# Messages, stores and sums of an attention stage sent in another order

## The chip, the cores and the metric

The kernel runs on one core of a Trainium2 chip. The metric is the device time of one execution in microseconds (us). The core's engines work side by side, each through its own list of instructions in order: PE (matrix products, with PEld for its weight loads), DVE, ACT and POOL (elementwise work) and SP, which here only issues DMAs and passes messages.

## The reference

```python
# attention, for each of 4 x 8 heads: 1152 keys, 64 wide
q_pool = q.reshape(B, H, S // 2, 2, D).mean(axis=3)          # 576 queries
scores = scale * np.matmul(q_pool, k.transpose(0, 1, 3, 2))  # 576 x 1152
attn = np.exp(scores - np.max(scores, axis=-1, keepdims=True))
attn = attn / (np.sum(attn, axis=-1, keepdims=True) + 1e-09)
x = np.matmul(attn, v)      # then the heads side by side: 2304 rows of 512
# first MoE block (dense): h = x @ w_in, g of h by pieces, x = g @ w_out (512 -> 2048 -> 512)
# second MoE block: each row to its best expert of 8, out = gate * (relu(x @ w1) @ w2)
```

## The kernel before

Attention takes the first 447 us of 1120; the two MoE blocks follow and are the same in both kernels. Its 32 heads go in 16 pairs, and a pair in nine steps of 128 queries; `s` counts all 144 steps, `t = s % 9` the steps of a pair, and step `t = 4` holds queries of both heads and has 18 score matmuls instead of 9. In a step PE makes the scores of 128 queries against 1152 keys into a PSUM tile `sc`, of which there is one (L238). DVE scales them into `e` and takes the peak of each row in the same instruction (L265). ACT takes the exponentials and their sums (L272). Two steps later PE transposes `e` in 64-wide pieces into `pa` and `pb` (L289); ACT and DVE split these into a high and a low part, `pth` and `ptl` (L307, L309), since every product is made of a few such parts. PE then multiplies them with `v` (L322, in four groups of 288 queries for a pair, of 36 half-row matmuls each), beside the scores of later steps. POOL splits q, k and v of the next pair (L180 to L214) and issues the loads of k.

All these matmuls use half the rows of the PE array (`UP` and `LO`), so that two run beside each other. Where both halves add into one PSUM bank, the second half's last part must come after the first half's end. `relay` (L254) sees to it with a nop on SP: the nop waits for the first half's last matmul, and the other half's matmul waits for the nop. This text calls it a message. Each step has one for the scores and one for the transposes; each group of L322 has one more.

SP takes its list in order, and the DMAs that it issues stand in the same list: loads of q (L153) and v (L165), stores of the products (`av_b` and `av_t`, L364), of the reciprocals of the sums (`rs_b`, L354) and loads of weights for the MoE block (L512, L517). `later` puts a DMA on a list with the step from which it may go, and at the end of each step `send` issues two of those that are due, or three at `t = 3` and in the last pair. `sums` (L344 to L354) makes the reciprocals of one pair's sums, transposes them on DVE and queues four small stores.

In the first three steps `warm` (L220) adds transposes whose result nobody reads: 22, 12 and 10 (`WARM`, L52). `load_first` (L132) loads q and k of the first two heads.

Near attention's end the MoE block's input `x` is read back from the stores. `tail` queues these loads: `xth` and `rows` with the upper and lower half of the products, `xtl` with the reciprocals, in two halves of 2 x 128 rows of the input, and a fifth part, `row`. POOL adds and multiplies them (L657, L658, L662), then issues the weights' third block (`raw`, L512). `h` of the MoE block (L692) follows on PE.

## Time and profile before

| | |
|---|---|
| three runs | 1118.53, 1121.33, 1123.40 us; median 1121.33 |
| profiled execution | 1121.47 us; span 1119.8 us |
| busy share of the span | PE 97%, PEld 89%, DVE 76%, ACT 67%, POOL 39% |
| DMA | 132.01 MB, mean 118 GB/s |
| granted TensorE clock | 0.993 of full speed, mean of the span |

The profile is of one execution, and its times are counted from the start of its span. A wait is idle time of an engine; behind the arrow stands what ended it, and `SPq L254` there is a message. The chain of waits goes back from the last instruction to whatever released each one. A row that begins with a number is an instruction or several of one kind in sequence, with the start and the duration.

### The profile page before, as it was taken

Reading aid. Unit: us, or ns where it says so; the run is one execution under the profiler, and the core shown is the slowest. Engines: PE = TensorE matmul, PEld = TensorE weight load, DVE = VectorE, ACT = ScalarE, POOL = GpSimd, SP = SyncE. Lnnn points to the kernel's source line nnn. Section 1 sums busy time; section 2 is a strip of 40 time slices with the busy share of each in tenths; the row PEclk is TensorE's granted clock in tenths of the full one; section 3 lists DMA queues with packets and bytes.
Section 4 is the critical chain, followed back from the end, with each engine's and each line's share of the span. In section 5 each row is a group of like instructions: output and inputs, shape, how many; then the busy total and the mean of one; then the engine's idle time right before and its main releaser. Section 6 shows DMA issues by size and latency. Waiting matters only on the chain.

```text
span 1119.8 us, 27167 instructions
## 1 busy us (share of the span) xinstructions
PE 1088.0 (97%) x10276; PEld 998.8 (89%) x10276; DVE 852.2 (76%) x1620; ACT 754.9 (67%) x1432; POOL 441.6 (39%) x473
## 2 busy tenths in 40 slices
PE   8999999999999998999999999999999999999997
PEld 7999989999889998999999989998889889988887
DVE  5999999999999995798757745663545866677775
ACT  4999989998898986555554445444446456577664
POOL 5988778778778848000021121101020231122211
PEclk8999999999999999999999999999999999999999
DMA  6445545446545435665132213210341121286544
GB/s 162 119 126 135 154 121 138 130 121 161 140 121 135 115 118 129 204 196 172 55 113 59 65 29 99 59 32 21 104 145 54 30 86 40 88 280 218 168 147 126
DMA packets 76854, 132.01 MB, mean 118 GB/s; under 512 B 21031, under 2 KB 39079, under 8 KB 76704
## 3 DMA queue, kind: packets, MB, share of 16 engines
q1 hardware_dynamic: 67856, 103.48, 31.9%
q0 software_dynamic: 8544, 26.31, 8.0%
q8 instruction: 88, 1.44, 0.6%
q14 instruction: 62, 0.51, 0.2%
q10 hardware_dynamic: 304, 0.26, 0.1%
HBM read 140.08 MB, written 20.08 MB: 143 GB/s over the span
## 4 chain that ended last, share of the span: by engine, by line
PE 73%; DVE 14%; issue 5%; POOL 2%; SPq 2%; DMA 2%; ACT 2%; POOLq 0%; DVEq 0%; ACTq 0%
PE h L692 18%; PE y L724 18%; PE sc L238 9%; DVE e L265 9%; PE d_po L1401 8%; PE d_ph L1367 7%; PE av L322 6%; DVE ptl L309 3%; PE pa L289 2%; PE d_ph L1381 1%; SPq L364 1%; DMA out<-d_ob,d_rec 1%; PE pb L289 1%; PE d_pt L1346 1%; POOL kT L193 1%
## 5 line engine op out<-in xcount | busy, mean ns | idle before, releaser
L265 DVE TENSOR_SCALAR_CACHE_REDUCE e<-sc 128x1152 f32<-128x1152 f32 x144 | 194.6, 1352 | 26.2 <-PE sc L238 23.1
L238 PE MATMUL sc<-kT,qt 64*128 64x384 f32 x1440 | 191.6, 350 | 18.5 <-DVE e L265 14.1
L272 ACT ACTIVATE e<-e,nm 128x1152 f32<-128x1152 f32 x144 | 182.2, 1265 | 8.6 <-DVE e L265 8.1
L238 PEld LDWEIGHTS sc<-kT,qt 64*128 64x128 f32 x1440 | 148.3, 187 | 35.9 <-DVE e L265 26.0
L1307 DVE TENSOR_TENSOR e<-e,e 128x512 fp32r<-128x512 f32 x200 | 129.9, 688 | 27.0 <-ACT e L1306 11.4
L322 PE MATMUL av<-pth,vh 64*128 64x288 f32 x1152 | 145.2, 311 | 2.3 <-SPq L254 2.2
L322 PE MATMUL av<-ptl,vh 64*128 64x288 f32 x1152 | 143.2, 311 | 0.0
L711 DVE SCALAR_TENSOR_TENSOR u<-h,u 128x320 f32<-128x320 f32 (+1 forms) x112 | 55.8, 498 | 113.3 <-ACT u L710 113.3
L309 DVE TENSOR_TENSOR ptl<-pa,pth 128x768 fp32r<-128x768 f32 x144 | 137.3, 953 | 4.3 <-ACT pth L307 3.4
L707 ACT ACTIVATE u<-h,half 128x320 f32<-128x320 f32 (+1 forms) x112 | 59.7, 533 | 118.5 <-PE h L692 116.9
L307 ACT CAST pth<-pa 128x768 fp32r<-128x768 f32 x144 | 114.9, 798 | 34.7 <-PE pa L289 32.3
L322 PEld LDWEIGHTS av<-pth,vh 64*128 64x128 f32 x1152 | 119.3, 186 | 4.3 <-SPq L254 4.3
L1401 PE MATMUL d_po<-e,e 128*128 128x512 f32 x504 | 120.6, 392 | 0.0
L322 PEld LDWEIGHTS av<-ptl,vh 64*128 64x128 f32 x1152 | 117.6, 186 | 0.0
L1306 ACT CAST e<-e 128x512 fp32r<-128x512 f32 x200 | 113.8, 620 | 0.3 <-issue 0.3
L724 PE MATMUL y<-wh,gh 128*128 128x512 f32 x288 | 113.9, 395 | 0.0
L724 PE MATMUL y<-wh,gl 128*128 128x512 f32 x288 | 113.7, 395 | 0.0
L724 PE MATMUL y<-wl,gh 128*128 128x512 f32 x288 | 113.6, 394 | 0.0
L1401 PEld LDWEIGHTS d_po<-e,e 128*128 128x128 f32 x504 | 92.8, 188 | 18.0
L289 PE MATMUL pb<-idf,e 64*128 64x64 f32 x864 | 100.6, 223 | 0.3
L657 POOL TENSOR_TENSOR xl<-xth,xl 128x512 f32<-128x512 f32 (+1 forms) x9 | 11.8, 1315 | 224.4 <-DMA xl<-av_b 127.2
L713 ACT CAST gh<-u 128x320 fp32r<-128x320 f32 (+1 forms) x112 | 52.4, 468 | 66.2 <-DVE u L711 66.1
(253 smaller groups left out, 2386.8 us busy)
## 6 DMA issues: line engine op xcount, KB each, us to landing
e<-moe_w SPq DMA_DIRECT2D x104, 512.0 KB
qr<-q SPq DMA_DIRECT2D x62, 288.0 KB
kr<-k POOLq DMA_DIRECT2D x60, 192.0 KB, 3.4
vr<-v SPq DMA_DIRECT2D x16, 576.0 KB
av_b<-avs SPq DMA_DIRECT2D x64, 128.0 KB
raw<-moe_w_in SPq DMA_DIRECT2D x14, 512.0 KB
raw<-moe_w_out SPq DMA_DIRECT2D x14, 512.0 KB
yt<-emb_rows SPq DMA_DIRECT2D x24, 256.0 KB
```

The source lines that it names most:

```text
L238: i = nc.tensor.matmul(s[:, j, 0:384], lhsT=qt[p, w, c:c + 128], rhs=d["kT", h][p, r], start=start, stop=stop)
L265: self.nc.vector.tensor_scalar(out=e.rearrange("p (a b) -> p a b", a=3), in0=d["sc"][:, :, 0:384], scalar1=-0.5 / D ** 0.5, scalar2=None, ...
L272: self.nc.scalar.activation(e, e, AF.Exp, bias=d["nm"][:, t:t + 1], scale=-1.0, accum_out=d["sum"][:, t:t + 1])
L289: x = nc.tensor.transpose(o, e[p, i * 128:(i + 1) * 128], idf[p, p])
L307: nc.scalar.copy(hi, p)
L309: nc.vector.tensor_sub(out=lo, in0=p, in1=hi.bitcast(F32))
L322: m = nc.tensor.matmul(box["t"][:, 0:GQ], lhsT=self.vh[p, h * 9 + i % 9], rhs=r[p, i % 9, c0:c0 + GQ], start=half == i == 0, stop=half == ...
L692: nc.tensor.matmul(ps[:, :n], lhsT=a[:, k], rhs=b[:, k, h0:h0 + n], start=i == 0, stop=i == 11)
L724: self.nc.tensor.matmul(y, lhsT=a, rhs=b, start=j == 0 and q == 0, stop=j == NF - 1 and q == 2)
L1306: self.nc.scalar.copy(hi, r)
L1307: self.nc.vector.tensor_sub(out=lo, in0=r, in1=hi.bitcast(F32))
L1401: self.nc.tensor.matmul(self.o, lhsT=(self.hh, self.hl)[a][f // 4][:, f % 4, s], rhs=self.w[b, f // 2][:, f % 2], start=f == 0 and q == 0, ...
```

## The change

The DMAs of attention go on two lists, stores first. One DMA is sent behind the scores' message, in the middle of the step, and one behind the transposes' message (two at `t = 3`, and at `t = 1` to `4` of the last pair). The reciprocals of two pairs are made together, behind the odd pair. At the start q of the second head and v of the first pair are loaded behind the first scores, k of the second head goes first, POOL's splits of the second head's q come a step later, and `WARM` has five portions. At attention's end the last transposes go into `sc`, and the last two groups of L322 become matmuls of whole rows, behind everything else (`av_all`). `tail` is called before the second `send` of its step, and the upper half of x is loaded in one piece of 512 x 512, with its reciprocals, ahead of both pieces of the lower half. ACT's and POOL's operations at the end follow in another order.

```diff
-WARM = 22, 12, 10
+WARM = 22, 12, 12, 8, 8
...
-    def later(self, step, f):
-        self.queue.append((step, f))
+    def later(self, step, f, queue=None):
+        (self.queue if queue is None else queue).append((step, f))
 
     def send(self, n):
-        out = [x for x in self.queue if x[0] <= self.step][:n]
-        for x in out:
-            self.queue.remove(x)
-            x[1]()
+        for q in (self.stores, self.queue):
+            out = [x for x in q if x[0] <= self.step][:n]
+            n -= len(out)
+            for x in out:
+                q.remove(x)
+                x[1]()
...
         if h:
-            parts = [(kr, ks), (qr, (q, q))]
+            parts = [(kr, ks)] if which == "k" else [(d["qr", h], (q, q))]
...
-    def turn(self, n, t):
+    def turn(self, n, t, late=False):
...
+        if late:
+            sc = self.ps_s.tile([128, 3, 512], F32, name="sc")
+            pa, pb = sc[:, 0:2], sc[:, 2:3]
...
+    def av_all(self, n, g):
+        h, c = g // 2, slice(g * GQ, g * GQ + GQ)
+        t = self.ps_v.tile([128, 512], F32, name="av", tag="av")
+        for i in range(18):
+            self.nc.tensor.matmul(t[:, 0:GQ], lhsT=self.vh[:, h * 9 + i % 9],
+                                  rhs=(self.pth if i < 9 else self.ptl)[:, i % 9, c], start=i == 0, stop=i == 17)
+        self.nc.scalar.copy(self.avs[:, c], t[:, 0:GQ])
+        if g % 2:
+            self.store(n, h)
...
     def sums(self, n):
 
         nc = self.nc
         del self.st[n]
+        if n % 2 == 0:
+            return
         b, hp = divmod(n, 4)
         rt = self.sm.tile([128, 32], F32, name="rt")
-        nc.vector.reciprocal(self.r[:, 0:9], self.r[:, 0:9])
+        nc.vector.reciprocal(self.r[:, 0:18], self.r[:, 0:18])
         nc.vector.transpose(rt, self.r)
...
         for c in range(4):
-            self.later(self.step + 1, lambda c=c: nc.sync.dma_start(out=out[c], in_=rt[32 * c:32 * c + 9]))
+            self.later(self.step + 1, lambda c=c: nc.sync.dma_start(out=out[c], in_=rt[32 * c:32 * c + 18]))
...
-                            self.later(s + (m > 1 and n == 0) * 4, lambda a=(m, h, p): self.load_q(*a))
-                if s < 3:
+                            self.later(s + (m > 1 and n == 0) * 3, lambda a=(m, h, p): self.load_q(*a))
+                if s < len(WARM):
                     self.warm(WARM[s])
                 up, lo = self.scores(n, t)
             for a in ready.get(s, []):
-                self.av_group(*a)
-            count = 18 if s > nt + 1 else 6 if t in (2, 3, 4) else 9
+                if a < (np_ - 1, 2):
+                    self.av_group(*a)
+            count = 18 if s >= nt else 6 if t in (2, 3, 4) else 9
...
             if s < nt:
                 self.peak(n, t)
+            if s == 0:
+                self.load_first(1, "q")
+                self.load_v(0)
+            self.send(1)
             if 2 <= s < nt + 2:
-                (a, b), ps = self.turn(*divmod(s - 2, 9))
-                if s >= nt:
-                    av(1, 4)
+                (a, b), ps = self.turn(*divmod(s - 2, 9), s > nt)
+                if s == nt:
+                    av(1, 7)
...
             go = s >= nt - 7 and len(g) > 0 and g[0][0]()
-            self.send(3 if t == 3 or n + 1 >= np_ else 2)
-            while any(min(left[half], len(self.avq[half])) for half in range(2)):
+            if s == nt - 9:
+                self.prep.release()
+                g.extend(tail())
+            self.send(2 if t == 3 or not more and 0 < t < 5 else 1)
+            while s != nt and any(min(left[half], len(self.avq[half])) for half in range(2)):
...
-            if s == nt - 1:
+            if s == nt + 1:
                 self.ps_s.release()
                 early()
-            if s == nt - 9:
-                self.prep.release()
-                g.extend(tail())
+                for a in range(2, 4):
+                    self.av_all(np_ - 1, a)
...
+                m1.x_raw(0, (slice(0, 4), 0, 512), lambda f: put(0, f))
                 for j in range(2):
                     part = slice(2 * j, 2 * j + 2), 0, 512
                     two = stage.tile([128, 1024], F32, name="rows", tag="m")
-                    m1.x_raw(0, part, lambda f, j=j: put(2 * j, f))
```

On SP, a stretch of ten DMAs of the steady state before. A wait for `PE_49` says that a message stands ahead of the DMA in the list; `DMAHW` is an earlier DMA on the same lane, `Pool` and `Activation` are these engines.

```order
L364 DMA av_b_72<-avs 64x512 [waits PE_49,DMAHW5_49,Activation_49]
L364 DMA av_t_76<-avs 64x64 [waits DMAHW6_49]
L364 DMA av_b_72<-avs 64x512 [waits PE_49,DMAHW7_49]
L364 DMA av_t_76<-avs 64x64 [waits DMAHW0_49]
L354 DMA rs_b_78<-rt 9x32 [waits DMAHW1_49,DVE_49]
L354 DMA rs_b_78<-rt 9x32 [waits PE_49,DMAHW2_49]
L354 DMA rs_b_78<-rt 9x32 [waits DMAHW3_49]
L354 DMA rs_b_78<-rt 9x32 [waits PE_49,DMAHW4_49]
L153 DMA qr_2177<-q 64x1152 [waits DMAHW5_49,Pool_49]
L153 DMA qr_2177<-q 64x1152 [waits PE_49,DMAHW6_49]
```

The stretch of the same pair after:

```order
L383 DMA av_b_72<-avs 64x512 [waits PE_49,DMAHW1_49,Activation_49]
L383 DMA av_t_76<-avs 64x64 [waits PE_49,DMAHW2_49]
L383 DMA av_b_72<-avs 64x512 [waits PE_49,DMAHW3_49]
L383 DMA av_t_76<-avs 64x64 [waits PE_49,DMAHW4_49]
L156 DMA qr_2064<-q 64x1152 [waits DMAHW5_49,Pool_49]
L156 DMA qr_2064<-q 64x1152 [waits PE_49,DMAHW6_49]
```

Each of the four stores now has a message of its own ahead of it, the four stores of reciprocals are gone from this pair, and the loads of q follow at once.

On PE, attention's end before: the last transposes (L289) and the last products with v (L322), which read `pth` and `ptl` in half rows.

```order
L289 MATMUL pa<-idf,e 128x64 x12
L322 MATMUL av<-ptl,vh 128x288
L289 MATMUL pb<-idf,e 128x64 x3
L322 MATMUL av<-ptl,vh 128x288 x8
L289 MATMUL pb<-idf,e 128x64 x3
L322 MATMUL av<-ptl,vh 128x288 x5
L322 MATMUL av<-pth,vh 128x288 x18
L322 MATMUL av<-ptl,vh 128x288 x18
L322 MATMUL av<-pth,vh 128x288 x9
L322 MATMUL av<-ptl,vh 128x288 x9
```

The same place after:

```order
L296 MATMUL sc<-idf,e 128x64 x12
L329 MATMUL av<-ptl,vh 128x288
L296 MATMUL sc<-idf,e 128x64 x3
L329 MATMUL av<-ptl,vh 128x288 x4
L296 MATMUL sc<-idf,e 128x64 x3
L329 MATMUL av<-ptl,vh 128x288
L351 MATMUL av<-pth,vh 128x288 x9
L351 MATMUL av<-ptl,vh 128x288 x9
L351 MATMUL av<-pth,vh 128x288 x9
L351 MATMUL av<-ptl,vh 128x288 x9
```

The transposes write `sc`, and behind them stand 36 matmuls of whole rows (L351) where half rows stood.

On POOL, the end of the chain on x before; `vh` is the split of v of the last head, `raw` the third block of weights.

```order
L662 TENSOR_TENSOR xtl<-rows,xth 128x512
L57 TENSOR_SCALAR vh<-vr 128x9x64
L214 TENSOR_TENSOR vh<-vr,vh 128x9x64
L657 TENSOR_TENSOR row<-xth,row 128x512
L658 TENSOR_TENSOR row<-row,xtl 128x512
L662 TENSOR_TENSOR xtl<-rows,xth 128x512 x2
L662 TENSOR_TENSOR xtl<-row,xth 128x4x128
L512 DMA raw<-moe_w_in 128x4x256
```

And after:

```order
L688 TENSOR_TENSOR xtl<-rows,xth 128x512
L683 TENSOR_TENSOR row<-xth,row 128x512
L684 TENSOR_TENSOR row<-row,xtl 128x512
L688 TENSOR_TENSOR xtl<-rows,xth 128x512
L57 TENSOR_SCALAR vh<-vr 128x9x64
L217 TENSOR_TENSOR vh<-vr,vh 128x9x64
L688 TENSOR_TENSOR xtl<-rows,xth 128x512
L688 TENSOR_TENSOR xtl<-row,xth 128x4x128
L538 DMA raw<-moe_w_in 128x4x256
```

The split of v has moved behind three operations on x.

## Rows read from the trace of the kernel before

**Rows 1.** Windows: length, busy PE, PEld, DVE, ACT, POOL (count), PEclk, DMA, GB/s.
```profile
100.00:400.00 300.00, 287.63 (x4501) 274.64 (x4499) 287.46 (x449) 270.86 (x467) 230.25 (x240) 1.00 0.49 129
```

**Rows 2.** Chain of waits, 30 to 445 us: shares by engine, operation, line.
```profile
by line: DVE e L265 23.2%; PE sc L238 23.1%; PE av L322 16.1%; DVE ptl L309 8.9%; PE pa L289 5.2%; issue 4.6%; SPq L364 2.8%; PE pb L289 2.5%; POOL kT L193 1.5%; ACT e L272 1.3%; POOL vh L214 1.2%; POOL qr L180 1.0%; DMA xtl<-rs_b 0.9%; ACT
```

**Rows 3.** Chain of waits inside one steady step: start us, us, what.
```profile
132.63 0.37 PE pa L289 x12
133.00 0.10 PE av L322
133.10 0.12 PE pb L289 x2
133.22 0.54 PE av L322 x8
```

**Rows 4.** Waits, 25 to 430 us (last two: 411 to 432): us, times, longest.
```profile
DVE e L265 <- PE sc L238: 16.5, 26, 1.9
...
PEld sc L238 <- SPq L254: 5.3, 12, 1.1
...
PEld av L322 <- SPq L254: 2.9, 4, 0.9
...
PEld sc L238 <- SPq L254: 2.2, 3, 1.1
...
PEld av L322 <- SPq L254: 0.9, 1, 0.9
```

**Rows 5.** Stores L364 on SP (least/median/most ns); timeline of one stall.
```profile
L364 SPq DMA_DIRECT2D av_b<-avs x64: 445/467/1612, 47.8 to 451.5; - x64
L364 SPq DMA_DIRECT2D av_t<-avs x64: 445/595/1561, 48.4 to 452.2; - x64
...
142.08 1.56 SPq L364 DMA_DIRECT2D av_t<-avs  x1
...
143.82 0.18 PEld L322 LDWEIGHTS av<-pth,vh 64*128 64x128 f32 x1 [0.74 <-SPq L254]
```

**Rows 6.** Timeline of DVE, 172 to 182 us: start, us, operation.
```profile
173.65 1.36 DVE L265 TENSOR_SCALAR_CACHE_REDUCE e<-sc 128x1152 f32<-128x1152 f32 x1
...
176.64 1.31 DVE L265 TENSOR_SCALAR_CACHE_REDUCE e<-sc 128x1152 f32<-128x1152 f32 x1
...
179.33 1.36 DVE L265 TENSOR_SCALAR_CACHE_REDUCE e<-sc 128x1152 f32<-128x1152 f32 x1
```

**Rows 7.** The start: timeline, one window (columns as rows 1), a chain row.
```profile
8.80 1.00 PE L238 MATMUL sc<-kT,qt 64*128 64x384 f32 x2 [1.09 <-SPq L254]
...
9.73 2.82 PE L220 MATMUL av<-idf 128*128 128x128 f32 x12
...
22.03 3.10 PE L238 MATMUL sc<-kT,qt 64*128 64x384 f32 x18 [0.39 <-DVE e L265]
...
22.00:25.60 3.60, 3.57 (x31) 3.49 (x32) 1.71 (x3) 1.60 (x4) 0.51 (x1) 0.53 1.02 232
...
100.96 2.01 PE sc L238 x18
```

**Rows 8.** Attention end: one window, then timeline of POOL, chain, DVE.
```profile
414.00:420.00 6.00, 5.63 (x81) 5.01 (x79) 5.38 (x8) 5.04 (x8) 0.70 (x2) 1.00 1.01 307
...
419.85 1.28 POOL L657 TENSOR_TENSOR rows<-xth,rows 128x512 f32<-128x512 f32 x1 [5.30 <-DMA rows<-av_b]
...
425.86 1.27 POOL L657 TENSOR_TENSOR rows<-xth,rows 128x512 f32<-128x512 f32 x1 [0.75 <-issue]
...
434.35 1.42 POOL L214 TENSOR_TENSOR vh<-vr,vh 128x576 fp32r<-128x576 f32 x1
...
442.08 0.82 POOL L512 DMA_DIRECT2D raw<-moe_w_in  x1
...
447.04 5.62 PE h L692 x36
...
448.59 0.43 DVE L561 TENSOR_SCALAR wf<-raw 128x512 uint32<-128x512 uint32 x1 [6.15 <-DMA raw<-moe_w_in]
```

More of the change, by code (lines that the diff above doesn't have):

```diff
@@ L84, in __init__ @@
         self.avq = [collections.deque() for _ in range(2)]
-        self.queue, self.full = [], []
-    def later(self, step, f):
-        self.queue.append((step, f))
+        self.queue, self.stores, self.full = [], [], []
+    def later(self, step, f, queue=None):
+        (self.queue if queue is None else queue).append((step, f))
     def send(self, n):
-        out = [x for x in self.queue if x[0] <= self.step][:n]
-        for x in out:
-            self.queue.remove(x)
-            x[1]()
+        for q in (self.stores, self.queue):
[4 more added lines that the diff above has]
+                x[1]()
     def open(self, ctx):
@@ L130, in source, with load_first @@
         return self.q[b, 2 * hp + h].rearrange("d (r q) -> d r q", r=2), (k[:, 0::2], k[:, 1:3])
-    def load_first(self, h):
+    def load_first(self, h, which):
         nc = self.nc
         d = self.st.setdefault(0, {})
-        qr = d["qr", h] = self.prep.tile([128, 2, NQ], F32, name=f"qr{h}")
-        kr = d["kr", h] = self.prep.tile([128, 2, S // 3], F32, name=f"kr{h}")
+        if "k" in which:
+            qr = d["qr", h] = self.prep.tile([128, 2, NQ], F32, name=f"qr{h}")
+            kr = d["kr", h] = self.prep.tile([128, 2, S // 3], F32, name=f"kr{h}")
         q, ks = self.source(0, h)
         if h:
-            parts = [(kr, ks), (qr, (q, q))]
+            parts = [(kr, ks)] if which == "k" else [(d["qr", h], (q, q))]
         else:
@@ L203, in split_qk @@
                           lambda: low(0, v, 1), lambda: low(0, v, 0)]
-                    + q(0, (g,) * 3, 128, 256) + q(0, (g,) * 3, 256) + q(1, (g,) * 3),
-                    [lambda: high(1, nc.scalar, None)], [lambda: low(1, v, 0), lambda: low(1, v, 1)], [])
+                    + q(0, (g,) * 3, 128, 256) + q(0, (g,) * 3, 256),
+                    q(1, (g,) * 3) + [lambda: high(1, nc.scalar, None)], [lambda: low(1, v, 0), lambda: low(1, v, 1)], [])
         nxt = [[lambda h=h: self.load_k(n + 1, h)] if n + 1 < self.NPAIR else [] for h in range(2)]
@@ L280, in turn @@
         idf = self.cn["idf"]
-        pa = self.ps_a.tile([128, 2, 512], F32, name="pa", tag="pa")
-        pb = self.ps_b.tile([128, 1, 512], F32, name="pb", tag="pb")
+        if late:
+            sc = self.ps_s.tile([128, 3, 512], F32, name="sc")
+            pa, pb = sc[:, 0:2], sc[:, 2:3]
+        else:
+            pa = self.ps_a.tile([128, 2, 512], F32, name="pa", tag="pa")
+            pb = self.ps_b.tile([128, 1, 512], F32, name="pb", tag="pb")
         last = {}
@@ L338, in av_group @@
         self.avq[0].extend(lambda j=j: mm(0, j) for j in range(18))
+    def av_all(self, n, g):
[7 more added lines that the diff above has]
+            self.store(n, h)
     def divisor(self, n):
         nc, d = self.nc, self.st[n]
-        nc.scalar.activation(self.r[:, 0:9], d["sum"], AF.Identity, bias=self.cn["eps"])
+        nc.scalar.activation(self.r[:, n % 2 * 9:n % 2 * 9 + 9], d["sum"], AF.Identity, bias=self.cn["eps"])
     def sums(self, n):
@@ L347, in sums @@
         del self.st[n]
+        if n % 2 == 0:
+            return
         b, hp = divmod(n, 4)
         rt = self.sm.tile([128, 32], F32, name="rt")
-        nc.vector.reciprocal(self.r[:, 0:9], self.r[:, 0:9])
+        nc.vector.reciprocal(self.r[:, 0:18], self.r[:, 0:18])
         nc.vector.transpose(rt, self.r)
-        out = self.xs.rs[b][hp].rearrange("(t c i) -> c t i", c=4, i=32)
+        out = self.xs.rs[b][hp - 1:hp + 1].rearrange("h (t c i) -> c (h t) i", c=4, i=32)
         for c in range(4):
-            self.later(self.step + 1, lambda c=c: nc.sync.dma_start(out=out[c], in_=rt[32 * c:32 * c + 9]))
+            self.later(self.step + 1, lambda c=c: nc.sync.dma_start(out=out[c], in_=rt[32 * c:32 * c + 18]))
     def store(self, n, h):
@@ L363, in store @@
                            (self.xs.av[B + b // 2][hp, s, p, b % 2 * 64:b % 2 * 64 + 64], rest)):
-                self.later(self.step + 1, lambda out=out, in_=av[:, c]: self.nc.sync.dma_start(out=out, in_=in_))
+                self.later(self.step + 1, lambda out=out, in_=av[:, c]: self.nc.sync.dma_start(out=out, in_=in_),
+                           self.stores)
     def run(self, aside, tail, early):
@@ L373, in run @@
             f()
-        self.load_v(0)
         self.load_k(1, 0)
@@ L387, in run @@
         s = -1
-        while s < nt + 1 or self.avq[0] or self.avq[1]:
+        while s < nt + 1:
             s += 1
@@ L479, in run @@
         self.step = nt * 2
-        self.send(len(self.queue))
+        self.send(len(self.stores) + len(self.queue))
         while g:
@@ L1558, in tile_kernel @@
                 nc.scalar.copy(at.qts[0][:, w, NQ:NQ + 64], zero)
-            for h in range(2):
-                at.load_first(h)
+            at.load_first(0, "qk")
+            at.load_first(1, "k")
             rt = Router(tc, one, dram, emb, tau, cn)
```

## The prediction

> **What bounds the kernel now.** I read the busy times of the steady stretch first, then the chain of waits, then the idle times by what ended them, and last the timelines of the three places that the change touches. Between 100 and 400 us PE and DVE are both busy for some 287.5 of 300 us, ACT for 271, at full TensorE clock [rows 1]. No engine has more than 12.5 us to give back there; what can be won is idle time that both share, or work taken off the one of the two that the chain is on. The chain of 30 to 445 us (415 us) goes by turns over DVE's peaks (23.2%), PE's scores (23.1%) and PE's sums over v (16.1%); SP's sequencer stands in it with 2.8% at the store line L364, which is 11.6 us [rows 2]. That share is the one that sending in another way can reach. A step lasts about 2.7 us (176.64 to 179.33 in [rows 6]).
>
> SP is in the chain because its nops are the messages that order the two half-row chains of a bank, and SP takes its list in order. A store's issue takes 0.45 us at best, 0.47 in the middle for the first of two and 0.60 for the second, and up to 1.61 and 1.56 [rows 5]. The example there: the second store of a batch is issued from 142.08 for 1.56 us, and PE's weight load at 143.82 has waited 0.74 us for a message behind it. From 25 to 430 us such waits come to 5.3 us before scores and 2.9 us before the sums over v, 16 of them [rows 4].
>
> **The change, part by part.** The sum is made against the profiled execution: 1121.47 us, a span of 1119.8 and 1.67 around it, 0.14 above the median of the three runs, so no correction between them is needed.
>
> *a. One DMA behind each message.* Before, two or three DMAs stand together at a step's end; after, one goes between the scores' message and the transposes' message, one behind the latter. Apart from b the number of DMAs and of messages stays, so SP's total is the same and only the longest row of issues before a message shrinks. What it can give back is bounded below by nothing (the stall moves to another message) and above by the 16.5 us that DVE's peaks idle for late scores, of which the stalls are one cause [rows 4]; the chain's 11.6 us lies between. I take the directly measured one: 5.3 + 2.9 = 8.2 us, less the 2.2 + 0.9 us of 411 to 432 us that belong to the tail (term d), is **5.1 us** [rows 4]. A single issue can still last 1.61 us and leave a stall, and the chain's larger share speaks for more; I let the two stand against each other.
>
> What the new place may cost: between the scores and the transposes' message PE has pa 0.37, av 0.10 and pb 0.12 us, and it needs the message only after another 0.54 us of av [rows 3]; that is 1.13 us, against an issue of 0.45 to 0.60. So I cost the place at nothing, and that cover is gone only when an issue with its own waits lasts over 1.13 us. Behind a held nop stand the second halves of pb on PE, and behind these ACT's and DVE's splits of the same step.
>
> *b. Sums of two pairs together.* Eight reciprocals and eight transposes leave DVE, and 32 of 64 small stores leave SP. The step with the sums takes 176.64 - 173.65 = 2.99 us from peak to peak against 2.69 us of the next [rows 6]: 0.30 us, so DVE has no room for them there. Seven of the eight that go lie before the tail: 7 x 0.30 = **2.1 us**. Bounds 1.0 (wider remaining reciprocals, some steps bound by PE) to 2.4 (all eight).
>
> *c. The start.* The first scores' message stands behind two loads of q and one of v, and PE waits 1.09 us for it at 8.80 [rows 7]. These go behind the scores: 1.0 us. The idle transposes gain two late portions of eight. From 22.0 to 25.6 us the clock was granted at 0.53 of full speed, which is the lower of its two levels, and the 18 score matmuls there took 3.10 us, against 2.01 at full speed at 100.96 [rows 7]: up to 1.1 us if the clock stays up. Each portion costs 8 x 2.82/12 = 1.9 us at the low clock and half of it, 0.9, at the high one [rows 7]; 0.39 us of idle time stood before the 18, so 0.5 shows, and as much for the other portion: a net 1.1 - 2 x 0.5 = 0.1. Together **1.1 us**, bounds -0.5 (the transposes do not hold the clock) to 3.5 (they also fill the earlier waits of the start).
>
> *d. Attention's end.* Before, POOL waits 5.30 us for its first rows of x, then runs from 419.85 to 442.08 with one gap of 0.75 us, and then issues the third block of weights [rows 8]. That block's split starts at 448.59 after a wait of 6.15 us, while PE's first h starts at 447.04: the x chain on POOL with the weights behind it and PE's attention end together [rows 8]. After, the load of x starts a step earlier (2.7 us), but in one piece: by the shapes in the code 1.05 (128 x 4 x 512 words of xth), 2 x 0.52 (xtl) and 0.52 (rows) = 2.62 MB must land before POOL's first operation, where it was 0.52 + 2 x 0.26 + 0.52 = 1.57 MB. At the 307 GB/s of 414 to 420 us, with the DMA engines busy throughout [rows 8], 1.05 MB more is 3.4 us: POOL starts 0.7 us later, and does without the gap of 0.75. The weights are issued as before. PE wins the 3.1 us of stalls left out above, but then waits for the weights; its last two groups as whole rows are 36 matmuls, and h's 36 took 5.62 us [rows 8], so they are no longer than what they replace by any margin that I can read. The split of v's last half, at 434.35 before [rows 8], stands three POOL operations later (some 3.8 us). So **0.0 us**, bounds -2 (PE waits for v or the weights by some part of those 3.8 us) to +5.8 (x lands early: the 2.7 us of the earlier step and PE's 3.1 us of stalls count in full).
>
> The Trainium skill ("DMA: Bandwidth & Descriptors", section "Where 436 GB/s comes from") puts what one core can draw from HBM at about 358 GB/s, by which the same 1.05 MB would be 2.9 us and the whole sum 0.5 us lower; the trace's 307 GB/s decides here.
>
> Sum: 5.1 + 2.1 + 1.1 + 0.0 = 8.3 us; 1121.47 - 8.3 = **1113.2 us**. With one term at a bound and the others as taken: a 1118.3 to 1101.8, b 1114.3 to 1112.9, c 1114.8 to 1110.8, d 1115.2 to 1107.4. What is late next: PE and DVE themselves, each busy for 96% of the steady stretch.
>
> **The rivals.**
>
> *A, the tail gains too.* If the whole piece of x lands as early as its issue, POOL's chain goes 2.7 us ahead and PE's 3.1 us count in full, 5.8 together: 1113.2 - 5.8 = 1107.4 us. For it: POOL's first operation waits for nothing but these loads, and the first of them is issued a step earlier; against it: the bytes ahead of that operation are two thirds more, on DMA engines that are busy throughout.
>
> *B, the order of sending gives nothing.* The stall only passes from the scores' message to the transposes' one, or the chain lies on DVE when SP is late: 1121.47 - 2.1 - 1.1 = 1118.3 us. For it: DVE is as busy as PE, so a gain of PE alone stays with PE; against it: DVE's peaks do wait 16.5 us for scores [rows 4], so the gain of PE is DVE's too. The Trainium skill ("DMA: Bandwidth & Descriptors", section "Issuing engines are not separate DMA queues") says that the sequencer time to initiate a DMA is usually small beside the DMA itself, which would make B the rule; this trace shows up to 1.61 us of it, and 8.2 us of waits behind it.
>
> *C, slower: the DMA in mid-step holds the transposes' message.* Place: the nop behind the first send. About 8 of a pair's 16 DMAs go there, 128 in all. An issue of 1.61 us against a cover of 1.13 holds PE for 0.48 us. If a third of them are so long, 43 x 0.48 = 20.5 us, and without term a: 1121.47 + 20.5 - 3.2 = 1138.8 us. It makes the kernel slower by over 0.5% from (5.6 + 3.2)/0.48 = 19 such issues on. For it: the long ones exist, and loads of q now go up to two steps earlier, nearer to POOL's last reading of their buffer. Against it: the long ones are rare, the middle of all first ones is 0.47 us.
>
> *D, PE waits at attention's end.* V's last split and the weights come late for a PE that has become early; it idles some 4 us, and may then run at the lower clock, as it did in [rows 7]: 1113.2 + 4 = 1117.2 us. For it: POOL's order; against it: PE must be early by more than 2 us first.
>
> **How the numbers follow.** The forecast has 0.54 (own range 1109 to 1117), A 0.17, B 0.14, C 0.08, D 0.07. Half a per cent is 5.6 us, about what a measurement here can tell from no change: faster means below 1115.7, slower above 1126.9. Faster: A's 0.17 and nine tenths of the forecast's, 0.49, together 0.66. Slower: C, and 0.01 for mishaps of the start: 0.09. Same: the rest, 0.25. The range goes from 1104 (beyond A, by the chain's 11.6 us in place of 5.1) to 1120 (B with its own spread); what is left out is C and the two far ends.
>
> **What the profile after would show.** a: PE's waits for the message nop between 25 and 410 us nearly gone, the share of SP's store line in the chain well under 2.8%, and steps of 2.7 us throughout; a is wrong if the same time stands before pb or before av. b: eight reciprocals on DVE, and seven steps of 2.7 in place of 2.99 us. c: the first scores about a microsecond earlier, and a granted clock near 1 from 22 to 26 us; if it is still 0.53 there, the portions cost 1 to 2 us. d: POOL's first operation on x at the same distance from the end of attention and the weights issued as late; if POOL starts 2 us or more ahead, A holds. A wait of the whole-row matmuls for v's split is D. The forecast is wrong if pairs of nine steps are not shorter than before, or if PE's waits for messages stay over 4 us.

## The result and the profile after

The changed kernel took 1109.43 us in the median of six runs, 1121.18 before: 11.8 us less, ratio 0.9896 (95% interval 0.9876 to 0.9916). Measured again beside the later experiments it was 1111.31 against 1119.44, ratio 0.9923 (0.9909 to 0.9938). The profiled execution took 1107.22 us, the shortest of the six, with a span of 1105.5. The profiled execution of the second measurement (e9) took 1113.39, the longest of its six; the two profiles lie on either side of what is usual.

The start times of the 144 peaks on DVE cut the span into four stages, which add up to it. Peak 9 is that of step `s = 9`, and the first y is PE's first matmul of the second product of the MoE block (its first product is `h`). Every stage is one profile's:

| kernel | to peak 9 | 9 to 135 | 135 to first y | first y to end | span |
|---|---|---|---|---|---|
| before | 38.79 | 368.83 | 46.91 | 665.27 | 1119.8 |
| changed | 34.25 | 360.06 | 46.28 | 664.91 | 1105.5 |
| changed, again (e9) | 34.43 | 360.53 | 52.02 | 664.62 | 1111.6 |

Of the profiled 14.3 us, 4.5 come from the start, 8.8 from the 126 steady steps, 0.6 from attention's end. In the second profile the end is 5.1 us longer than before.

The steady stretch, as [rows 1], [rows 2] and [rows 4] have it of before: busy times of 100 to 400 us, the chain from 30 to 394 us, and the waits of 25 to 394 us (us, times, longest).

```profile
100.00:400.00 300.00, 290.71 (x4628) 281.22 (x4626) 294.25 (x452) 276.81 (x482) 233.74 (x243) 1.00 0.51 131
...
by line: PE sc L241 29.4%; DVE e L268 25.8%; PE av L329 21.2%; DVE ptl L316 8.2%; PE pa L296 5.8%; issue 3.8%; PE pb L296 3.1%; DVE wf L595 0.5%; DVE wf L591 0.4%; DVE rt L370 0.4%; DVE r L369 0.4%; ACT e L275 0.3%; DVE wf L587 0.2%; ACT pt
...
DVE e L268 <- PE sc L241: 3.1, 9, 0.8
...
PEld pb L296 <- SPq L257: 0.3, 1, 0.3
```

DVE is now busy for 294 of 300 us instead of 287, and PE waits 0.3 us for messages in the whole stretch. SP is not in the row of the chain, whose shares go down to 0.2%. DVE's peaks idle 3.1 us for scores. In the kernel before it was, from 25 us to its own peak 135 (407 us), so without the tail that [rows 4] has in its 16.5:

```profile
DVE e L265 <- PE sc L238: 13.3, 21, 1.9
```

Then the stores' issue on SP (least/median/most ns), which answers to [rows 5]:

```profile
L383 SPq DMA_DIRECT2D av_b<-avs x64: 445/459/597, 39.0 to 434.8; - x64
L383 SPq DMA_DIRECT2D av_t<-avs x64: 445/467/1132, 40.4 to 435.5; - x64
```

The median of av_t, which was the second of a pair, went from 595 to 467 ns: the issues did not only move, they became shorter.

A step with sums and one without, DVE's timeline, as [rows 6]:

```profile
165.10 1.36 DVE L268 TENSOR_SCALAR_CACHE_REDUCE e<-sc 128x1152 f32<-128x1152 f32 x1
...
167.72 0.25 DVE L369 RECIPROCAL r<-r 128x18 f32<-128x18 f32 x1
...
168.14 1.32 DVE L268 TENSOR_SCALAR_CACHE_REDUCE e<-sc 128x1152 f32<-128x1152 f32 x1
...
190.78 1.36 DVE L268 TENSOR_SCALAR_CACHE_REDUCE e<-sc 128x1152 f32<-128x1152 f32 x1
...
193.50 1.36 DVE L268 TENSOR_SCALAR_CACHE_REDUCE e<-sc 128x1152 f32<-128x1152 f32 x1
```

With sums 3.04 us from peak to peak, without them 2.72: the eighteen columns' reciprocal takes 0.25 us, and the step with it is 0.05 longer than the 2.99 of before.

The start, as [rows 7]: PE's first and fifth scores, and the windows from 8 us on (columns as rows 1); the last row is the first window in the kernel before.

```profile
6.69 1.38 PE L241 MATMUL sc<-kT,qt 64*128 64x384 f32 x8 [0.28 <-ACT kT L59]
...
18.60 1.85 PE L241 MATMUL sc<-kT,qt 64*128 64x384 f32 x18
...
8.00:14.00 6.00, 5.82 (x58) 5.03 (x57) 4.16 (x7) 3.55 (x6) 5.37 (x7) 1.00 1.05 276
22.00:26.00 4.00, 4.00 (x58) 3.97 (x59) 4.00 (x7) 3.82 (x7) 3.75 (x5) 1.00 0.02 5
...
8.00:14.00 6.00, 5.20 (x23) 4.38 (x23) 1.37 (x2) 2.07 (x3) 3.54 (x5) 0.55 0.87 220
```

The first scores end without a wait for a message, and the clock is granted in full in both windows, where it was 0.55 from 8 to 14 us before.

Attention's end, as [rows 8]: SP's loads of x, the waits of POOL, PE and DVE, and a window.

```profile
395.20 0.39 SPq L641 DMA_DIRECT2D xth<-av_b  x1
...
403.31 0.37 SPq L672 DMA_DIRECT2D rows<-av_b  x1
...
407.86 4.27 SPq L641 DMA_DIRECT2D xtl<-rs_b  x4
...
409.17 1.29 POOL L683 TENSOR_TENSOR rows<-xth,rows 128x512 f32<-128x512 f32 x1 [8.32 <-DMA rows<-av_b]
...
430.62 0.82 POOL L538 DMA_DIRECT2D raw<-moe_w_in  x1
...
411.54 0.69 PE L241 MATMUL sc<-kT,qt 64*128 64x384 f32 x1 [1.61 <-SPq L257]
...
433.08 0.75 PE L718 MATMUL h<-xth,wh 128*128 128x320 f32 x4
...
435.50 0.43 DVE L587 TENSOR_SCALAR wf<-raw 128x512 uint32<-128x512 uint32 x1 [4.71 <-DMA raw<-moe_w_in]
...
410.31:414.31 4.00, 2.77 (x31) 2.78 (x33) 1.95 (x3) 2.16 (x4) 3.84 (x4) 0.63 0.33 76
```

Counted from peak 135 (407.62 before, 394.31 after), POOL's first operation on x comes at 14.9 us instead of 12.2, the weights' issue at 36.3 instead of 34.5. PE waits 1.61 us for a message that stands behind the loads of x, and the clock falls to 0.63 for a while.

### The profile page after: what moved, and what is told of

The parts are those of the page before. It is cut to its first block, busy times and chain, and to the rows that moved or that the text cites. A ratio compares the mean times of both kernels' runs of the same rounds, so it can differ in the third digit from the quotient of the medians.

```text
span 1105.5 us, 27077 instructions
## 1 busy us (share of the span) xinstructions
PE 1079.8 (98%) x10258; PEld 996.5 (90%) x10258; DVE 848.4 (77%) x1604; ACT 752.8 (68%) x1432; POOL 443.9 (40%) x473
## 4 chain that ended last, share of the span: by engine, by line
PE 77%; DVE 12%; issue 5%; DMA 3%; POOL 2%; ACT 1%; POOLq 0%; SPq 0%; DVEq 0%; ACTq 0%
PE h L718 18%; PE y L750 18%; PE sc L241 11%; DVE e L268 9%; PE d_po L1427 7%; PE av L329 7%; PE d_ph L1393 7%; DVE ptl L316 3%; PE pa L296 2%; PE d_ph L1407 1%; PE pb L296 1%; DMA out<-d_ob,d_rec 1%; PE d_pt L1372 1%; DMA xth<-av_b 1%; POOL rows L683 0%
## 5 line engine op out<-in xcount | busy, mean ns | idle before, releaser
L268 DVE TENSOR_SCALAR_CACHE_REDUCE e<-sc 128x1152 f32<-128x1152 f32 x144 | 195.1, 1355 | 16.3 <-PE sc L241 11.7
L241 PE MATMUL sc<-kT,qt 64*128 64x384 f32 x1440 | 183.0, 345 | 14.3 <-DVE e L268 11.4
L241 PEld LDWEIGHTS sc<-kT,qt 64*128 64x128 f32 x1440 | 145.9, 184 | 27.8 <-DVE e L268 22.5
L329 PE MATMUL av<-pth,vh 64*128 64x288 f32 x1116 | 140.9, 313 | 0.1
L329 PE MATMUL av<-ptl,vh 64*128 64x288 f32 x1116 | 137.3, 310 | 0.0
L329 PEld LDWEIGHTS av<-pth,vh 64*128 64x128 f32 x1116 | 116.9, 188 | 0.5 <-SPq L257 0.3
L329 PEld LDWEIGHTS av<-ptl,vh 64*128 64x128 f32 x1116 | 112.9, 186 | 0.0
```

The lines of the kernel that those rows point to most:

```text
L241: i = nc.tensor.matmul(s[:, j, 0:384], lhsT=qt[p, w, c:c + 128], rhs=d["kT", h][p, r], start=start, stop=stop)
L268: self.nc.vector.tensor_scalar(out=e.rearrange("p (a b) -> p a b", a=3), in0=d["sc"][:, :, 0:384], scalar1=-0.5 / D ** 0.5, scalar2=None, ...
L329: m = nc.tensor.matmul(box["t"][:, 0:GQ], lhsT=self.vh[p, h * 9 + i % 9], rhs=r[p, i % 9, c0:c0 + GQ], start=half == i == 0, stop=half == ...
```

## The experiments

All are edits of the changed kernel, but for e6, an edit of the kernel before, and e9, the changed kernel itself. Ratios are to the kernel before on the same chip. Stages are those of the table above. The changed kernel's own ratio, for comparison, is 0.9896 or 0.9923. A stage is read from one profile. The start and the steady steps of the changed kernel agree within 0.5 us in its two profiles, but its stage from peak 135 to the first y took 46.28 and 52.02 us, and 50.86 and 52.64 in e3 and e4, which leave that stage alone; so differences of a few us in this stage are weak by themselves.

| run | median us | ratio (interval) | to peak 9 | 9 to 135 | 135 to first y |
|---|---|---|---|---|---|
| e1_batch | 1117.55 | 0.9961 (0.9946 to 0.9976) | 34.54 | 370.07 | 50.66 |
| e2_sums | 1113.91 | 0.9921 (0.9898 to 0.9945) | 34.78 | 361.43 | 52.86 |
| e3_first | 1114.46 | 0.9927 (0.9903 to 0.9952) | 37.30 | 360.03 | 50.86 |
| e4_warm | 1112.96 | 0.9922 (0.9900 to 0.9943) | 34.12 | 360.74 | 52.64 |
| e5_xhalf | 1111.63 | 0.9926 (0.9906 to 0.9947) | 34.35 | 360.28 | 49.39 |
| e6_spread | 1116.54 | 0.9970 (0.9957 to 0.9984) | 39.16 | 361.22 | 50.09 |
| e7_poolx | 1117.78 | 0.9981 (0.9965 to 0.9997) | 35.22 | 360.51 | 55.63 |
| e8_half | 1116.64 | 0.9968 (0.9952 to 0.9984) | 34.31 | 360.15 | 55.72 |
| e9_after | 1111.31 | 0.9923 (0.9909 to 0.9938) | 34.43 | 360.53 | 52.02 |
| e10_best1 | 1104.10 | 0.9860 (0.9842 to 0.9879) | 34.38 | 361.12 | 42.83 |
| e11_best2 | 1103.88 | 0.9858 (0.9839 to 0.9877) | 34.30 | 362.04 | 41.83 |

**e1_batch: the spacing undone.**

```diff
-            self.send(1)
...
-            self.send(2 if t == 3 or not more and 0 < t < 5 else 1)
+            self.send(3 if t == 3 or not more else 2)
```

> The changed kernel with its DMAs sent as before, two (three at t = 3 and in the last pair) together at the end of the step, and all else as changed. Theory (the spacing of the DMAs behind the messages gave the steady part of the gain): pairs 1 to 14, which became 8.8 us shorter in the profile, give back that less the 2.1 us of the sums, some 6.7 us: 1109.4 + 6.7 = about 1116 us (1114 to 1118); PE's waits for messages between 25 and 394 us, now 0.3 us, are back at 4 to 6, and stores that take over 1 us to issue are back. Rival (the spacing gave nothing; the steady gain comes from stores first, earlier loads of q or POOL's order): 1109 to 1110 us, pairs stay at 25.7 us on average.

The steady steps took 370.07 us, 10.0 more than in the changed kernel, though everything else in them was left as changed. Its waits of 25 to 404 us and its stores:

```profile
DVE e L268 <- PE sc L241: 11.7, 20, 1.5
...
PEld sc L241 <- SPq L257: 5.4, 9, 0.8
...
PEld av L329 <- SPq L257: 1.2, 3, 0.6
...
L383 SPq DMA_DIRECT2D av_t<-avs x64: 445/596/1657, 41.1 to 450.2; - x64
```

Waits for messages are back at 6.6 us, the long issues too, and DVE's idling for scores at 11.7. The theory holds, the rival falls. The direct waits are less than what the stage lost: 6.6 of 10.0. DVE's idling for scores rose by 8.6 us, which is nearer.

**e6_spread: the spacing alone, on the kernel before.** The edit is `later`, `send` and the two calls of `send` of the change, the stores' list, and `* 3` for `* 4` at the loads of q.

> The kernel before with one part alone: stores first, one DMA behind each message (two at t = 3 and at t = 1 to 4 of the last pair), and loads of q for pair 2 a step earlier. Start, sums, WARM, x and attention's end stay as before. Theory (the spacing is the larger part of the steady gain): the steady 126 steps (9 to 135) take 361 to 363 us instead of 368.8, and the time is 6 to 7 us below before, ratio 0.994. Rival (spacing helps only with fewer DMAs, because the sums of each pair fill the slots): 366 us or more, ratio 0.998.

The steady steps took 361.22 us, 7.6 less than before, with the sums still made for each pair. The ratio is only 0.9970, for the end lost 3.2 us (46.91 to 50.09). So the gain of the steps was as expected, and the time was not: 4 us below before, not 6 to 7. On PE and DVE, what the end lost:

```profile
445.31 1.26 PE L696 MATMUL h<-xth,wh 128*128 128x320 f32 x4 [4.47 <-DVE u L715]
...
DVE wf L565 <- DMA raw<-moe_w_in: 12.2, 1, 12.2
```

The first h comes at 36.6 us after peak 135 instead of 39.4, but the weights, which POOL issues behind its work on x, go out at 38.9 us instead of 34.5: DVE waits 12.2 us for them with the rest of its list behind, and PE 4.47 us for DVE, which it did not before. That is rival D's late weights, without a change at attention's end.

**e2_sums: a pair's sums by themselves.** The edit takes back `divisor` and `sums`.

> The changed kernel with reciprocals, transpose and four stores for each pair, as before. Theory (each of the eight extra places on DVE costs its 0.30 us, seven of them before the tail): 1109.4 + 2.1 = 1111.5 us; the step with the sums is some 3.0 us in every pair. Rival (with messages in time DVE has room): under 0.7 us, 1109.4 to 1110.1. Second rival (32 more DMAs, one per message, make loads late): over 4 us, 1113.5 or more, with waits on loads of q or v that the changed kernel does not have.

The steady steps took 361.43 us: 1.4 more than in the changed kernel's first profile, 0.9 more than in its second. That lies between theory and rival; no load came late. The ratio can't tell so little.

**e3_first: the first loads in the old place.**

```diff
+        self.load_v(0)
         self.load_k(1, 0)
...
-            if s == 0:
-                self.load_first(1, "q")
-                self.load_v(0)
...
             at.load_first(1, "k")
+            at.load_first(1, "q")
```

> The changed kernel with the first loads in the old place: q of the second head and v of the first pair are issued ahead of the first scores, so the first message stands behind them. Theory (the clock fell in the kernel before because PE waited for that message): the first peak is back at about 9.8 us from 8.1, the granted clock between 8 and 14 us is back near 0.55, and 3 to 4.5 us are lost: about 1113 us. Rival (the two more portions of idle transposes hold the clock by themselves, the message costs its wait alone): clock at or near 1.00, loss 1.0 to 1.7 us, about 1111 us.

PE's wait for the message and the window behind it:

```profile
8.67 0.62 PE L241 MATMUL sc<-kT,qt 64*128 64x384 f32 x2 [1.26 <-SPq L257]
...
8.00:14.00 6.00, 5.33 (x29) 4.50 (x30) 1.94 (x3) 2.07 (x3) 5.18 (x8) 0.72 1.05 269
```

Peak 9 comes 3.05 us later than in the changed kernel, and the clock falls to 0.72 behind a wait of 1.26 us, with all five portions of idle transposes in place. The theory holds in the trace of this stage, though less of it came back than expected (the first peak at 9.33 us, not 9.8; the clock at 0.72, not 0.55). The other profiles agree: in the three with these loads ahead of the first message (before, e6, e3) the clock of 8 to 14 us is 0.55, 0.55 and 0.72, in the ten others 1.00. The whole time (0.9927 against 0.9896 and 0.9923) is too coarse to show it.

**e4_warm: 22, 12 and 10 idle transposes.**

```diff
-WARM = 22, 12, 12, 8, 8
+WARM = 22, 12, 10
```

> The changed kernel with idle transposes in three portions of 22, 12 and 10 as before. Theory (the first message alone kept the clock up): clock at 1.00 from 8 to 22 us still, and the time the same or up to 1 us shorter, since 18 transposes are gone: 1108.5 to 1109.5 us. Rival (the fourth and fifth portion are what holds the clock through the scores of t = 4): the clock falls to about 0.55 for some 3 us between 18 and 24 us and 1.1 to 2.8 us are lost: 1110.5 to 1112.2 us.

```profile
8.00:14.00 6.00, 5.53 (x55) 4.73 (x55) 4.25 (x7) 3.65 (x6) 5.36 (x7) 1.00 0.99 263
18.00:22.00 4.00, 3.45 (x52) 3.14 (x49) 3.36 (x7) 3.81 (x8) 3.89 (x5) 1.00 0.94 235
```

The clock stays at 1.00, and peak 9 comes at 34.12 instead of 34.25 us. With the first message in time the 18 transposes were neither needed nor a cost. Whether they help when that message is late no run shows: in e3, which has them, the clock is back at 1.00 from 14 us on, and in the kernel before, which has not, it is 0.82 from 14 to 18 us and 0.57 from 22 to 26, but the two differ in more than that. The ratio of 0.9922 is next to e9's 0.9923; the 1108.5 to 1109.5 expected of the theory were counted from the first measurement. The time above them lies in the end (52.64 us), which this edit does not touch.

**e9_after: the changed kernel once more.**

> The changed kernel once more, beside the two versions below on one chip. Theory (its tail depends on when the 1 MB piece of x lands, and the first profile was a lucky one): ratio 0.990 to 0.993, POOL's first operation on x 15 to 20 us after the peak of step 135, the first h 39 to 45 us after it, and a stretch at the lower clock in between. Rival (the first result is the usual one, and the experiments lost by their own edits): ratio 0.9896 and the tail as in the first profile.

The theory holds in all its parts: ratio 0.9923, POOL's first operation at 19.0 us after peak 135, the first h at 44.5, and a stretch at the lower clock. SP's issues around the second piece of rows, two waits of SP from 390 to 420 us, PE and POOL's waits, and two windows:

```profile
402.66 0.45 SPq L383 DMA_DIRECT2D av_t<-avs  x1
406.14 0.37 SPq L672 DMA_DIRECT2D rows<-av_b  x1
409.64 0.36 SPq L641 DMA_DIRECT2D xth<-av_t  x1
...
SPq L641 <- DMA xtl<-rs_b: 5.8, 2, 3.1
...
SPq L672 <- DMA xth<-av_b: 2.1, 1, 2.1
...
410.12 0.94 PE L241 MATMUL sc<-kT,qt 64*128 64x384 f32 x3 [3.60 <-SPq L257]
...
413.98 1.29 POOL L683 TENSOR_TENSOR rows<-xth,rows 128x512 f32<-128x512 f32 x1 [12.49 <-DMA rows<-av_b]
...
400.96:404.96 4.00, 3.64 (x58) 3.16 (x54) 3.97 (x7) 3.68 (x6) 0.53 (x1) 1.00 1.08 167
408.96:412.96 4.00, 2.85 (x28) 2.85 (x29) 1.44 (x3) 0.80 (x1) 0.00 (x0) 0.66 0.99 286
```

The store at 402.66 is issued in 0.45 us, and the load of rows behind it only at 406.14, three microseconds later; the next at 409.64. In SP's list of the changed kernel these wait for DMAs issued eight places ahead:

```
L641 DMA xth<-av_b_72 128x4x512 [waits PE_49,DMASW5_49,DMASW4_49,DMASW6_49,DMASW3_49,DMASW7_49,DMASW2_49,DMAHW7_49,DMASW1_49,DMASW0_49]
...
L672 DMA rows<-av_b_72 128x2x512 [waits PE_49,DMAHW7_49,DVE_49]
L641 DMA xth<-av_t_76 128x4x128 [waits DMAHW0_49]
```

Lane 7 is that of the 1 MB piece of x, lane 0 that of its first 0.5 MB of reciprocals. Until such a piece has landed SP stands still, the message behind it with SP, and PE with the message: 3.60 us, then the clock at 0.66. The rows of SP's waits say the same: 2.1 us for the 1 MB piece, and more, 5.8 us in two waits, for reciprocals; PE's 3.60 us stand behind one of the latter. That the wait is for the lane is read from the list; no run took the lane alone away.

**e5_xhalf: x in two halves again.**

```diff
-                m1.x_raw(0, (slice(0, 4), 0, 512), lambda f: put(0, f))
...
                     two = stage.tile([128, 1024], F32, name="rows", tag="m")
+                    m1.x_raw(0, part, lambda f, j=j: put(2 * j, f))
```

> The changed kernel with the upper half of x loaded in two halves, each with its reciprocals, as before; the spacing of the DMAs stays. Theory (in the changed kernel the second piece of rows has to wait on SP until the 1 MB piece of x, eight DMAs ahead of it, has landed, and a message stands behind it): PE's longest wait for a message after step 135 falls from 1.6 to 4.2 us to under 1 us, POOL's first operation on x comes at 12 to 14 us after the peak of step 135 instead of 15 to 20, the clock stays at 1.00 there, and 3 to 6 us are won over the changed kernel's usual tail: about 1106 us (ratio to before 0.985 to 0.988). Rival (the piece is no matter, POOL's chain or the weights end the tail either way): ratio 0.9896 as the changed kernel.

What was expected of the place came, and POOL even earlier: it starts 10.6 us after peak 135, PE's waits for messages come to 0.3 us, the clock stays at 1.00 up to the first h, and that comes at 33.7 us instead of 38.8 (changed) or 44.5 (e9). But little of it reached the end, which took 49.4 us against e9's 52.0:

```profile
436.94 0.43 DVE L587 TENSOR_SCALAR wf<-raw 128x512 uint32<-128x512 uint32 x1 [10.54 <-DMA raw<-moe_w_in]
...
437.82 1.44 PE L718 MATMUL h<-xth,wh 128*128 128x320 f32 x4 [4.24 <-DVE u L737]
...
438.63:442.63 4.00, 4.00 (x17) 4.00 (x16) 3.69 (x8) 2.51 (x6) 0.00 (x0) 0.50 0.80 271
...
429.50 1.28 POOL L688 TENSOR_TENSOR xtl<-rows,xth 128x512 fp32r<-128x512 f32 x1 [3.08 <-ACT xth L687]
...
431.98 0.82 POOL L538 DMA_DIRECT2D raw<-moe_w_in  x1
```

POOL issues the weights behind all its work on x, at 431.98. DVE waits 10.54 us for them and PE 4.24 us for DVE, then PE runs at the lower clock (0.50). The expected ratio of 0.985 to 0.988 was missed (0.9926): the wait for the weights had been hidden by the ones that went, as in e6. The ten profiles in which the weights stand last on POOL and PE does not wait long for v's split (all but e8, e10 and e11) bear this out: the first y comes 10.0 to 12.8 us after POOL issues the weights, though that issue lies anywhere from 34.5 to 43.4 us after peak 135.

**e7_poolx: the loads of x issued by POOL.** The edit puts `(self.nc.gpsimd if g == 0 else self.nc.sync)` for `self.nc.sync` in `x_raw` and `x_load`.

> The changed kernel with the loads of the first group of x issued by POOL instead of SP, in the same pieces. Theory (the tail's stalls are messages behind these loads on SP): PE's waits for messages after step 135 fall to under 1 us in all, the clock stays at 1.00, though the loads themselves are as large; POOL's chain starts when they land, so 1 to 4 us are won over the changed kernel's usual tail, ratio 0.986 to 0.989. Rival (the loads' landing and POOL's chain are the limit, and POOL's issues cost it 1 us each): no gain or 1 to 3 us lost, ratio 0.990 to 0.992, with PE waiting for POOL at the end instead.

```profile
ACT xth L687 <- POOL rows L684: 9.1, 4, 4.4
...
417.98 0.90 PE L296 MATMUL pa<-idf,e 64*128 64x64 f32 x12 [5.14 <-DVE ptl L316]
```

The messages' waits are gone (0.3 us in all), as the theory had it. The rest of it failed: the clock fell in this stage too (0.50 from 431.73 to 439.73 us), and the end became 3.6 us longer than in e9, more than the rival's 1 to 3: POOL starts at 17.3 us, ACT has a cast of x in its list ahead of the splits of the transposes and waits 9.1 us for POOL, DVE for ACT, and PE 5.14 us for DVE. So late landing of the large piece has a second way to hold PE, through ACT's order. And it lands late without SP: from the issue of its first load at 395.51 to POOL's first operation it is 17.5 us, against 18.1 in e9.

**e8_half: attention's end in half rows.** The edit takes back the conditions of `run` for the last steps, and `av_all` and `late` with them.

> The changed kernel with attention's end as before: the last two groups in half rows with messages, no transposes into the scores' bank, and the scores' pool released at step 143. Theory (the whole-row form costs and saves nothing that can be read): within 1.5 us of the changed kernel, ratio 0.988 to 0.991. Rival (the half rows end earlier because they start before the split of v's last half): 2 to 3 us faster. Second rival (the whole rows save messages and steps): 2 to 3 us slower, ratio 0.992.

```profile
431.39 1.33 PE L329 MATMUL av<-pth,vh 64*128 64x288 f32 x7 [3.95 <-POOL vh L217]
```

And in e9, with whole rows:

```profile
433.06 1.69 PE L351 MATMUL av<-pth,vh 128*128 128x288 f32 x9 [1.89 <-POOL vh L217]
```

The end took 55.7 us, 3.7 more than in e9, and the ratio is 0.9968 against 0.9923: more than the second rival gave it. It does not come from messages, for which PE idles 2.9 us behind peak 135 against 4.1 in e9: PE comes to the last group earlier and waits 3.95 us for the split of v, which POOL makes later in this order. The whole rows hide a part of that, 1.89 us are left in e9.

**e10_best1 and e11_best2: x in halves and the weights earlier.** x in halves as in e5, the third block's w_in issued as soon as its buffer is free, and in e11 the last casts of x ahead of the last products:

```diff
-                        (lambda: True, [lambda: one(3), lambda: evs[1]()]),
+                        (lambda: True, [lambda: one(3), lambda: evs[1](), lambda: rest(0)]),
...
-                        (lambda: True, [lambda: evs[3]()]), (lambda: True, [lambda: evs[4](), rest])]
+                        (lambda: True, [lambda: evs[3]()]), (lambda: True, [lambda: evs[4](), lambda: rest(1)])]
...
+            if go:
+                for f in g.popleft()[1]:
+                    f()
+            if s == nt + 1:
                 for a in range(2, 4):
                     self.av_all(np_ - 1, a)
-            if go:
-                for f in g.popleft()[1]:
-                    f()
```

> The changed kernel with the upper half of x in two halves, and the third block's w_in issued by POOL as soon as the first rows' buffer is free, in front of the split of v's last half, its w_out at the end as before. Theory (with x in halves the only thing late is that block: PE idled 4.2 us for it, and then ran at the lower clock): the first h starts 33 to 34 us after the peak of step 135, the first y 41 to 43 us after it instead of 46 (changed kernel) and 49 (x in halves alone), and 5 to 8 us are won over x in halves: ratio 0.985 to 0.988, 1104 to 1107 us. Rival (the weights' split on DVE or the last splits of x on POOL take the wait's place): no more than 2 us won, ratio 0.991.

> The same, and in the last step the casts and splits of x are put ahead of the last two groups of products, on ACT and PE's list alike. Theory (with x in halves POOL waited 3.1 us for ACT's cast behind the copies of the last products): POOL's last split comes some 3 us earlier, PE's waits of 0.5 us before the first h are gone, 0.5 to 1.5 us are won over the version before it. Rival (the casts then hold ACT's last copies, and the products' bank with them): the same or 1 us slower.

The first h and the first y of e11, on PE (peak 135 is at 396.34):

```profile
430.66 0.76 PE L719 MATMUL h<-xth,wh 128*128 128x320 f32 x4
...
438.17 0.40 PE L751 MATMUL y<-wh,gh 128*128 128x512 f32 x1
```

From peak 135 to the first y it is 42.8 and 41.8 us instead of 46.9 before and 46.3 to 52.0 in the changed kernel, and the clock stays at 1.00 from there to the first y. The numbers of e10 all came as expected. The ratios, 0.9860 and 0.9858, lie below the changed kernel's, and their intervals below that of e9 on the same chip: 7 us won. The casts' order (e11 against e10) won 1.0 us in this stage and nothing that the median can tell. The weights' earlier issue without x in halves was not run, so how much of the 7 us needs both is open.

## Why the prediction was right, and where not

The direction and the range held: 1109.4 us in a range of 1104 to 1120, faster by 1.04% where 0.7% was forecast (0.77% in the second measurement). The terms behind it were less good. It was not rival A, near as its 1107.4 lies: POOL did not start earlier but later.

*a, spacing: right in kind, too small.* Forecast 5.1 us; the spacing was worth 7.6 us by itself (e6) and 10.0 us at the changed kernel (e1). The step that failed is "I take the directly measured one": PE's idling for messages is less than what a late message costs. What followed the stage's time better is the row that was taken as the upper bound, DVE's idling for scores: it fell by 8.7 us with the spacing alone (13.3 to 4.6, e6) and rose by 8.6 without it (3.1 to 11.7, e1). The chain's 11.6 us includes the tail; from 30 to 407 us its store line has 2.2%, 8.3 us. A part of the gain is that the back-to-back issues were themselves longer than single ones; how the rest arises was not taken apart. That the place in mid-step costs nothing held in the steady steps (0.3 us of waits). B is refuted by e1 and e6. The rule of the Trainium skill ("DMA: Bandwidth & Descriptors", section "Issuing engines are not separate DMA queues") would have made it the outcome. Its words compare an issue with its DMA. The traces show what counts here: how long the issues ahead of a message last beside the 1.13 us of work that PE has in [rows 3] until it needs it. One issue takes 0.45 to 0.6 us, and the second of two up to 1.66.

*b, sums: right in kind, at most two thirds of the size.* 0.9 to 1.4 us instead of 2.1. The failed step is that the sums that stay cost nothing more, which only the lower bound allowed for: the seven steps without sums are 0.26 us shorter on average, near the 0.30 forecast, but the seven that keep them became 0.05 longer, together 1.5 us.

*c, the start: a quarter of its size.* 4.5 us instead of 1.1, above the bound of 3.5. The failed step is the one that priced the message's wait at its 1.09 us and gave the clock to the idle transposes. The low clock of 8 to 14 us followed from that wait: with the wait put back it fell again (e3, 3.05 us), with the transposes taken back it did not (e4). The remaining 1.5 us between e3 and the kernel before go with a clock that was low for longer there (also 14 to 18 and 22 to 26 us); why, was not taken apart.

*d, attention's end: forecast 0.0; +1.0 us in the first profile, -4.5 in the second (from peak 135 to the end of the span).* The failed step is "POOL starts 0.7 us later": it was 2.6 and 6.8 us. A window's rate is not the pace at which one piece arrives. From the issue of the first load of x (in the kernel before the row below) to POOL's first operation at 419.85 it took 8.62 us for 1.57 MB, 182 GB/s:

```profile
411.23 0.39 SPq L615 DMA_DIRECT2D xth<-av_b  x1
```

At that pace 1.05 MB more are 5.8 us, and POOL would start 3.1 us later, near the 2.6 of the first profile; the issue itself came 2.7 us earlier, as forecast. In e9 the piece took 18.1 us, 145 GB/s. The rate of 307 GB/s did not hold there either; with the DMA engines busy throughout, e9 shows 167 GB/s in one window and 286 in another. And the loads of x did what rival C said of the mid-step DMA, only there and not in the steps: one issue with its own wait held a message, PE idled for up to 3.60 us, and the clock fell as in D. D's wait for v's split itself was 0.33 us in the first profile and 1.89 in e9. I had weighed the bytes before POOL's first operation and not who waits on SP behind them. The 358 GB/s of the Trainium skill ("DMA: Bandwidth & Descriptors", section "Where 436 GB/s comes from") is shown by none of these windows; the measured rates decide. Nor is it a bound in these traces: a window of the kernel before, 459.62 to 463.62 us, has 369 GB/s.

That the sum came near is luck. For a and b together, c and d the first profile has 8.8 + 4.5 + 1.0 = 14.3 us and the second 8.3 + 4.4 - 4.5 = 8.2, against 7.2 + 1.1 + 0.0 = 8.3: in the second two terms that were too small stand against one that was too favourable, in the first the gain is 1.7 times the forecast.

## What to carry to other kernels

Where one engine's list carries both transfers and the signals that others wait for, count its issues between two signals, not only its total: one behind each signal was worth 2 to 3% of the steady steps (e6, e1). A transfer in that list can also wait for an earlier one to land. Smaller pieces took that wait away here (e5); another engine's list took it from PE's messages too, but the large piece then held PE by way of ACT (e7). And when a stall is removed, look at once for what was hidden behind it: x in halves won nothing that the ratio shows until the weights were issued earlier.

## What the runs showed of the hardware that was not expected

The issue of a DMA on SP took longer right behind another: the small store av_t had a median of 595 ns (before) and 596 ns (e1) as the second of a pair, and 467 ns where it was spaced. Of its issues from 40 to 400 us, 11 of 54 (before) and 10 of 55 (e1) took over 1 us, all of them right behind another DMA; of the spaced ones (changed kernel, e9, e6) none did. One wait of 1.1 to 1.3 us of PE near the start was followed by the lower clock (0.55 to 0.72 in the windows), while dropping 18 idle transposes changed nothing where that wait was gone. The same kernel moved its data at the same place at different rates, on DMA engines that show busy throughout (shares 1.00 to 1.06): in the two windows of 4 us from 4 to 12 us after peak 135 it was 301 and 215 GB/s in the first profile and 260 and 164 in e9.
